# Pieces of weight forms moved into the first half of each plain chunk of a spectral block with a GeGLU FFN

## The chip, the cores and the metric

The kernel runs on one core of one Trainium2 chip. The core has five engines that run their own queues of instructions in order and meet through semaphores: TensorE (PE in the profile, with its weight loads as PEld), VectorE (DVE), ScalarE (ACT), GpSimd (POOL) and SyncE (SP), which here only issues DMAs. The metric is the device time of one execution in microseconds (us), the median of several runs. The three runs shown of the kernel before took 1930.48 to 1935.18 us.

## What is computed

One block of a network with two residual branches, over 8192 tokens of 448 channels:

```python
x = A_x
mod = (_silu(c) @ w_mod).reshape(c.shape[0], 6, 1, -1)
sa, ca, ga, sb, cb, gb = (mod[:, 0], mod[:, 1], mod[:, 2], mod[:, 3], mod[:, 4], mod[:, 5])
h = _layernorm(x, axis=-1) * (1 + ca) + sa
x = x + ga * _A_ref(h, A_w1, A_b1, A_w2, A_b2)
h = _layernorm(x, axis=-1) * (1 + cb) + sb
x = x + gb * _B_ref(h, B_w_gate, B_w_up, B_w_down)
return x
```

`_A_ref` is a spectral layer: a two-dimensional Fourier transform over tokens, a small complex two-layer network on blocks of 112 channels, soft shrinkage, and the inverse transform. `_B_ref` is the FFN, `(_gelu(x @ w_gate) * (x @ w_up)) @ w_down`, with 1792 hidden features. The change touches only the FFN's part of the program.

## The kernel before

**Stages.** First come the layernorm, the transforms and the spectral network (to about 387 us of the profiled execution). Then the FFN runs over 32 chunks of 256 tokens (two groups of 128, `CB = 2`). The first eight, chunks 0 to 7 (`NSTD = 8`), are the *plain chunks*; chunks 8 to 31 use a scheme with seven products in place of eight for a 2x2 block product in gate and up as well, and need other *forms* of the gate and up weights: sums and differences of blocks, each as a high and a low half-precision part. The weights have seven tiles (`NP = 7`), and in plain chunk 1 + n the forms of tile n are built, piece by piece, between the chunk's own work.

**A plain chunk** has 14 steps (k = 0 to 13, `NFT = 14`). In each, `gate_up(i, k)` (L1118 for its matmuls) writes one bank of PSUM, and `gate_up_out` empties it: ScalarE takes the gelu of the gate half (L1154), VectorE multiplies it with the up half (L1159), and that multiply frees the bank. Banks go in pairs of two steps (`pgu`, tags `pa` and `pb`, two buffers each), so four steps are in flight. After each second step GpSimd makes four sums of the product (`sums`, L1167 to L1170), and `quantize` makes its high part on ScalarE (L1178) and the low part on VectorE (L1179). Behind step 2 stand the *down products* of the chunk before (`down`: L1191 to L1193, 147 matmuls in seven products): ScalarE copies two of them out (L1218, L1224), VectorE adds the others (L1219, L1227, L1228, L1232, L1233, L1238), and GpSimd finishes the chunk from L1234 on (L1205, L1206). `down` calls a hook `mid` at three places among the products, written m0, m1, m2 in the tables.

**The next chunk but one is prepared in the same steps** (tables `hooks`, and `soon` for chunks 6 and 7): step 3 splits its spectral values and transform (`split_g`, `split_v`: L113 on ScalarE, L115 on GpSimd); step 6 does the inverse transform on TensorE (`inverse`: L1018 to L1020, of which L1020 needs the last split, `v`); step 7 the residual (`residual`: L1029 on VectorE, L1030 on GpSimd); then the statistics (L1038, L1041), the reciprocal root (L124 to L133), the normalise (`norm2`: L1067, L1068) and the pack (L1073, L1080 to L1082). For chunks 8 and 9 the pack is another: `token_sums` (L1294 to L1300), `wpack_hi` on ScalarE (L1321) and `wpack_lo` on GpSimd (L1327).

**The forms of a weight tile**, by the table `prep`: `load_forms` fetches the raw weights (`wr`, L1513); `form_sums` makes two pairs of sums on GpSimd (part 0: L1522 and L1523; part 1: L1525 and L1526, which overwrites what some pieces read); ten pieces follow, each `forms_hi` on ScalarE (L1556) and `forms_lo` on VectorE (L1561), piece 4 with one more copy (L1564); `store_forms` writes the result (`ws`) to memory in two parts, four DMAs each (L1570). The order on each engine is the order in which the tables call these functions (a schedule written by hand), so an engine waits at the first instruction that is not ready.

**The change of stage.** Behind chunk 7 the plain stage's memory and PSUM pools are closed. The first matmuls of the new stage (L1350, tile `set`) wait until all plain banks are free; then `copy_b` on ScalarE (L1378, tile `sb`) copies their result, and the next matmuls wait for that copy.

Of the kernel before, what the change touches and what calls it, by code (L numbers as in the profile page):

```python
# [32 lines left out]
NFT = F // 128  # L33
# [7 lines left out]
NSTD = 8  # L41
# [8 lines left out]
def spectral_geglu(ctx, tc, x, w1, b1, w2, b2, wg, wu, wd, cvec, wmod, cf1, cs2, cmi, cgm, out):  # L50
# [91 lines left out]
    with ExitStack() as actx:  # L142
# [147 lines left out]
        pe, start = 0.0, {}  # L290
# [684 lines left out]
    with ExitStack() as cctx:  # L975
# [342 lines left out]
        def wpack_hi(i, ks):  # L1318
            for k in ks:
                for src, hi, _ in pieces(i, k):  # L1320
                    S.copy(hi, src)  # L1321
# [111 lines left out]
        held = []  # L1433
# [61 lines left out]
            6: [(2, wpack_hi, [4]), (2, wpack_lo, [4]), (3, load_g)],  # L1495
        }

        def pack(i):
            pack_hi(i)
            pack_lo(i)  # L1500
# [65 lines left out]
        def store_forms(t, part):  # L1566
            w = raws.pop(("s", t, part))
            for pr, rows in enumerate(rows2):
                for r, c in zip(rows2, range(2)):
                    dma(wk[t][part][r, pr], w[rows, :, c::2])  # L1570

        prep = {}
        for n in range(NP):
            for k, fn, *args in (
                (0, load_forms),
                ("m0", form_sums, 0),
                ("m0", forms_hi, 0),
                ("m1", forms_lo, 0),
                ("m1", forms_hi, 2),
                ("m2", forms_lo, 2),  # L1580
                ("m2", forms_hi, 1),
                (3, forms_lo, 1),
                (4, forms_hi, 3),
                (5, forms_lo, 3),
                (5, forms_hi, 4),
                (6, forms_lo, 4),
                (7, form_sums, 1),
                (7, forms_hi, 5),
                (8, forms_lo, 5),
                (8, forms_hi, 6, 7),  # L1590
                (8, store_forms, 0),
                (9, forms_lo, 6, 7),
                (10, forms_hi, 8),
                (11, forms_lo, 8),
                (11, forms_hi, 9),
                (12, forms_lo, 9),
                (13, store_forms, 1),
            ):
                at_k = (n, NFT - 1) if k == 0 and n else (1 + n, k)
                prep.setdefault(at_k, []).append((fn, n, *args))  # L1600
        for n, k in enumerate((4, 7, 11, 13)):
            for part in range(2):
# [10 lines left out]
            11: [(2, norm2, 0)],  # L1613
            12: [(2, norm2, 1)],
            13: [(2, pack)],
        }

# [6 lines left out]
        }  # L1624

        soon = {
            5: [(1, turn)],
            3: [(2, split_g), (2, split_v)],
            6: [(2, inverse)],
            7: [(2, residual)],  # L1630
            8: [(2, stats2), (2, rsqrt_part, 5)],
            9: [(2, rsqrt_part, 9), (2, norm2, 0)],
            10: [(2, norm2, 1), (2, token_sums, 0), (2, wpack_hi, [0, 1]), (2, wpack_lo, [0, 1])],
            11: [(2, token_sums, 1), (2, wpack_hi, [2]), (2, wpack_lo, [2])],
            12: [(2, wpack_hi, [3]), (2, wpack_lo, [3])],
            13: [(2, wpack_hi, [4]), (2, wpack_lo, [4])],
        }

        ahead = {
# [110 lines left out]
        for u in range(U0, NT_ + 1):  # L1750
            period(u)
            i, k = divmod(u, NP)
# [95 lines left out]
```

## Time and profile before

| what | value |
|---|---|
| runs shown, median (lowest to highest) | 1933.28 us (1930.48 to 1935.18) |
| the profiled execution, its own time | 1934.03 us |
| its span, first to last instruction | 1931.7 us |
| mean granted clock of TensorE | 0.989 |
| TensorE busy | 1862.0 us (96%) |
| VectorE, ScalarE, GpSimd busy | 1417.0, 995.3, 1261.5 us |
| plain chunks (first to last L1118) | 386.8 to 790.0 us |
| chunks 8 to 31 | from 798.1 us on |

How to read it: the profile counts an engine as busy while it executes, not while it waits; instructions have the line of the kernel that issued them. In the order of time a row gives start, duration, engine, line, operation, what it writes and reads, and in brackets how long the engine idled before it and what ended that. A row of a table by stage gives the stretch, its length, busy time and count of instructions for PE, PEld, DVE, ACT and POOL, the clock granted to TensorE, the DMA share and GB/s. Chunk numbers are worked out from the order: 308 matmuls of L1118 make one plain chunk.

### The profile page before, as it was taken

To read this page: it belongs to the slowest core of one execution; us is meant where nothing else is said; L and a number is where in the kernel's file an instruction comes from. 1 tells how busy PE (TensorE), PEld (TensorE's weight loads), DVE (VectorE), ACT (ScalarE), POOL (GpSimd) and SP (SyncE) were. 2 spreads that over 40 slices of the span, in tenths; PEclk is the share of its full clock that TensorE was granted. 3 is DMA by queue.
4 is the path that set the end of the run, shared out by engine and by line. 5 is a ranking of instruction groups with operands and counts; after the bars stand their busy time and mean duration, and the time that the engine had idled before them with its cause. 6 is when DMAs were issued, how large, how long until landed. Compare 5 with 4: busy or idle time off the path is not lost.

```text
span 1931.7 us, 56478 instructions
## 1 busy us (share of the span) xinstructions
PE 1862.0 (96%) x23332; PEld 1757.8 (91%) x23332; DVE 1417.0 (73%) x2888; ACT 995.3 (52%) x1843; POOL 1261.5 (65%) x1616
## 2 busy tenths in 40 slices
PE   7899999899999999799999999999999999999998
PEld 3599999778888887699999999999999999999998
DVE  8677788777555565577777777777777777777645
ACT  5687888553333333344444555555555555454443
POOL 3157654247777776577777777777777777777533
PEclk9899999999999999899999999999999999999999
DMA  9999777553434444976665666666565666666651
GB/s 351 315 286 259 200 185 195 163 138 79 101 100 101 100 101 111 247 192 171 168 164 165 164 173 181 169 181 180 167 165 164 164 167 182 168 178 178 157 160 53
DMA packets 380602, 330.49 MB, mean 171 GB/s; under 512 B 110772, under 2 KB 358712, under 8 KB 380344
## 3 DMA queue, kind: packets, MB, share of 16 engines
q1 hardware_dynamic: 380344, 326.87, 61.3%
q8 instruction: 183, 3.00, 0.6%
q14 instruction: 75, 0.61, 0.1%
HBM read 243.32 MB, written 60.10 MB: 157 GB/s over the span
## 4 chain that ended last, share of the span: by engine, by line
PE 72%; DVE 14%; DMA 4%; ACT 4%; POOL 3%; issue 2%; SPq 1%; ACTq 0%; POOLq 0%; DVEq 0%
PE set L1350 36%; PE pdn L1193 6%; PE pdn L1191 6%; PE pdn L1192 6%; PE pgu L1118 4%; PE ps L210 2%; PE set L1193 2%; PE set L1192 2%; PE set L1191 2%; DVE y L471 2%; DVE ws L1561 1%; DVE ac L1179 1%; DVE x L1159 1%; POOL x L1030 1%; DVE wk L824 1%
## 5 line engine op out<-in xcount | busy, mean ns | idle before, releaser
L1350 PE MATMUL set<-nt,wk 128*128 128x128 f16 x13104 | 745.4, 219 | 12.7 <-DVE x L1159 8.1
L1350 PEld LDWEIGHTS <-wk 128*128 128x128 f16 x13104 | 738.3, 98 | 17.9 <-issue 15.9
L1193 PE MATMUL pdn<-wd,ac 128*128 128x224 f16 x1218 | 315.5, 259 | 1.7 <-DVE ac L1425 1.2
L1191 PE MATMUL pdn<-wd,ac 128*128 128x224 f16 x1218 | 315.7, 259 | 0.8 <-ACT ac L1415 0.6
L1192 PE MATMUL pdn<-wd,ac 128*128 128x224 f16 x1218 | 315.5, 259 | 0.0
L1118 PE MATMUL pgu<-nt,wk 128*128 128x256 f16 (+1 forms) x2464 | 274.6, 275 | 19.0 <-DVE x L1159 18.9
L1118 PEld LDWEIGHTS <-wk 128*128 128x128 f16 (+1 forms) x2464 | 227.1, 98 | 65.1 <-issue 38.5
L1399 ACT ACTIVATE gl<-c,dg 128x384 f32<-128x384 f32 x168 | 103.5, 616 | 254.4 <-DVE c L1393 253.3
L1425 DVE SCALAR_TENSOR_TENSOR ac<-x,sa_act,ac 128x896 f16<-128x896 f32 x168 | 212.5, 1265 | 14.8 <-ACT ac L1415 14.7
L1167 POOL TENSOR_TENSOR x<-x 128x128 f32<-128x128 f32 x223 | 135.4, 607 | 122.0 <-DVE x L1159 82.9
L1234 POOL TENSOR_TENSOR o<-u,p 128x224 f32<-128x224 f32 x32 | 21.1, 659 | 278.5 <-DVE u L1233 278.5
L1403 DVE TENSOR_TENSOR x<-c,gl 128x384 f32<-128x384 f32 x168 | 176.2, 1049 | 17.1 <-ACT gl L1399 17.1
L1415 ACT ACTIVATE ac<-x,sa_act 128x896 f16<-128x896 f32 x168 | 173.7, 1034 | 3.5 <-DVE x L1170 0.4
L1170 POOL TENSOR_TENSOR x<-x 128x128 f32<-128x128 f32 x223 | 171.3, 768 | 0.0
L1191 PEld LDWEIGHTS <-ac 128*128 128x128 f16 x1568 | 153.4, 98 | 5.7 <-issue 4.7
L1193 PEld LDWEIGHTS <-ac 128*128 128x128 f16 x1568 | 153.4, 98 | 2.7 <-DVE ac L1425 1.7
L1192 PEld LDWEIGHTS <-ac 128*128 128x128 f16 x1568 | 153.5, 98 | 0.4 <-issue 0.4
L1169 POOL TENSOR_TENSOR x<-x 128x128 f32<-128x128 f32 x223 | 146.3, 656 | 0.0
L1387 DVE TENSOR_TENSOR c<-set,sb 128x512 f32<-128x512 f32 x168 | 115.0, 685 | 42.5 <-PE set L1350 42.5
L1168 POOL TENSOR_TENSOR x<-x 128x128 f32<-128x128 f32 x223 | 117.3, 526 | 17.5
L471 DVE SCALAR_TENSOR_TENSOR y<-pm,t 64x224 f32<-64x224 f32 x256 | 99.5, 389 | 39.0 <-ACT t L463 35.1
L115 POOL TENSOR_TENSOR yl<-y,yh 128x448 fp32r<-128x448 f32 x63 | 76.7, 1218 | 73.5 <-ACT yh L113 60.2
(323 smaller groups left out, 3948.4 us busy)
## 6 DMA issues: line engine op xcount, KB each, us to landing
wk<-wk SPq DMA_DIRECT2D x76, 1024.0 KB, 6.4
wk<-wk SPq DMA_DIRECT2D x76, 768.0 KB, 5.0
tr<-td SPq DMA_DIRECT2D x64, 224.0 KB, 4.6
vd<-us SPq DMA_DIRECT2D x64, 224.0 KB, 3.1
xx<-in_A_x SPq DMA_DIRECT2D x32, 448.0 KB, 4.9
v<-vd SPq DMA_DIRECT2D x63, 224.0 KB, 4.8
out<-x SPq DMA_DIRECT2D x31, 448.0 KB, 4.1
xt<-in_A_x SPq DMA_DIRECT2D x15, 896.0 KB, 16.4
```

The costliest lines, as they stand in the source:

```text
L471: V.scalar_tensor_tensor(y[ri * 64 : ri * 64 + 64, gi], pv[si, ri], LAM, tv[si, ri], op0=ALU.add, op1=ALU.min)
L1118: T.matmul(pgu[i, t, q][:, pr * H : (pr + 1) * H], ws[rows, n, w, tw], nts[i][rows, tn, :], start=start, stop=stop, skip_group_check=True,)
L1167: e.tensor_tensor(s1, a21, a22, ALU.add)
L1169: e.tensor_tensor(s3, a11, a21, ALU.subtract)
L1170: e.tensor_tensor(s4, a12, s2, ALU.subtract)
L1191: T.matmul(ps, ac[:, 0, ka], w[:, 0, kb], start=n == 0, stop=False)
L1192: T.matmul(ps, ac[:, 0, ka], w[:, 1, kb], start=False, stop=False)
L1193: T.matmul(ps, ac[:, 1, ka], w[:, 0, kb], start=False, stop=n == NP - 1)
L1350: T.matmul(ps2[:, pr, reg * 128 : reg * 128 + 128], slot[:, pr, hl, wt, :], nt[:, xt, :], start=start and j == 0, stop=j == len(terms) - 1 ...
L1403: V.tensor_tensor(xs[u][:, 1::3, :], cts.pop(u)[:, 1], gls.pop(u), ALU.mult)
L1415: S.activation(ac[:, 0], xs[u][:, 0:7], AF.Copy, scale=sa_act[:, t : t + 1])
L1425: V.scalar_tensor_tensor(ac[:, 1], xs.pop(u)[:, 0:7], sa_act[:, t : t + 1], ac[:, 0], op0=ALU.mult, op1=ALU.subtract)
```

## The change

The table `prep` is split in two, `start` for tile 0 (in chunk 1) and `steady` for tiles 1 to 6 (in chunks 2 to 7). In `steady` the raw weights are loaded at step 8 of the chunk before (six steps before its end) in place of step 13; the first form sums stand at step 0, the pieces 0 and 2 at steps 0 to 2, pieces 1, 3, 4 and 5 at the hooks m0 to m2 among the down products, the second form sums at m2, and the rest at steps 3 to 6; the stores move from steps 8 and 13 to 3 and 7. For chunks 8 and 9 (table `soon`) the normalise moves to steps 10 and 11, the token sums and the first pack pieces to 12 and 13, and `pack_rest` packs the last two pieces, for chunk 9 in the first period of the new stage.

```diff
+        def pack_rest(i):
+            if i == NSTD:
+                wpack_hi(i, [3, 4])
+                wpack_lo(i, [3, 4])
+            else:
+                held.extend([(f, i, [k]) for k in (3, 4) for f in (wpack_hi, wpack_lo)])
...
+        start = [
+            (0, load_forms),
+            ("m0", form_sums, 0),
+            ("m0", forms_hi, 0),
+            ("m1", forms_lo, 0),
+            ("m1", forms_hi, 2),
+            ("m2", forms_lo, 2),
+            ("m2", forms_hi, 1, 3),
+            (3, forms_lo, 1, 3),
+            (3, forms_hi, 4),
+            (4, forms_lo, 4),
+            (4, form_sums, 1),
+            (4, forms_hi, 5),
...
+            (8, forms_lo, 9),
+            (9, store_forms, 1),
+        ]
+        steady = [
+            (-6, load_forms),
+            (0, form_sums, 0),
+            (0, forms_hi, 0),
+            (1, forms_lo, 0),
+            (1, forms_hi, 2),
+            (2, forms_lo, 2),
+            (2, forms_hi, 1),
+            ("m0", forms_lo, 1),
+            ("m0", forms_hi, 3, 4),
+            ("m1", forms_lo, 3),
+            ("m1", forms_hi, 5),
+            ("m2", forms_lo, 4, 5),
+            ("m2", form_sums, 1),
+            ("m2", forms_hi, 6, 7),
+            (3, store_forms, 0),
+            (3, forms_lo, 6, 7),
+            (4, forms_hi, 8),
+            (5, forms_lo, 8),
+            (5, forms_hi, 9),
+            (6, forms_lo, 9),
+            (7, store_forms, 1),
+        ]
         prep = {}
         for n in range(NP):
-            for k, fn, *args in (
-                (0, load_forms),
-                ("m0", form_sums, 0),
-                ("m0", forms_hi, 0),
-                ("m1", forms_lo, 0),
-                ("m1", forms_hi, 2),
-                ("m2", forms_lo, 2),
-                ("m2", forms_hi, 1),
-                (3, forms_lo, 1),
-                (4, forms_hi, 3),
-                (5, forms_lo, 3),
-                (5, forms_hi, 4),
-                (6, forms_lo, 4),
-                (7, form_sums, 1),
-                (7, forms_hi, 5),
-                (8, forms_lo, 5),
-                (8, forms_hi, 6, 7),
-                (8, store_forms, 0),
-                (9, forms_lo, 6, 7),
-                (10, forms_hi, 8),
-                (11, forms_lo, 8),
-                (11, forms_hi, 9),
-                (12, forms_lo, 9),
-                (13, store_forms, 1),
-            ):
-                at_k = (n, NFT - 1) if k == 0 and n else (1 + n, k)
+            for k, fn, *args in steady if n else start:
+                at_k = (n, NFT + k) if type(k) is int and k < 0 else (1 + n, k)
...
         soon = {
...
-            9: [(2, rsqrt_part, 9), (2, norm2, 0)],
-            10: [(2, norm2, 1), (2, token_sums, 0), (2, wpack_hi, [0, 1]), (2, wpack_lo, [0, 1])],
-            11: [(2, token_sums, 1), (2, wpack_hi, [2]), (2, wpack_lo, [2])],
-            12: [(2, wpack_hi, [3]), (2, wpack_lo, [3])],
-            13: [(2, wpack_hi, [4]), (2, wpack_lo, [4])],
+            9: [(2, rsqrt_part, 9)],
+            10: [(2, norm2, 0)],
+            11: [(2, norm2, 1)],
+            12: [(2, token_sums, 0), (2, wpack_hi, [0, 1]), (2, wpack_lo, [0, 1])],
+            13: [(2, token_sums, 1), (2, wpack_hi, [2]), (2, wpack_lo, [2]), (2, pack_rest)],
         }
```

In the changed kernel the same operations have other line numbers: the pieces are L1563 (ScalarE) and L1568 (VectorE) with the copy L1571, the form sums L1529, L1530 and L1532, L1533. Three places show how the order moves.

VectorE in chunk 4, from the fifth down product (`u`) to step 3, before (`ws` are the pieces, `o` and `u` the down products, `x` the gate/up product, `ac` its quantised form):

```order
L1228 TENSOR_TENSOR u_8613<-pdn,u_8612 128x224
L1561 SCALAR_TENSOR_TENSOR ws<-wr,sww,ws 128x3x128
L1232 TENSOR_TENSOR o<-pdn,u_8613 128x224
L1233 TENSOR_TENSOR u_8612<-pdn,u_8612 128x224
L1238 TENSOR_TENSOR o<-pdn,u_8613 128x224
L1159 TENSOR_TENSOR x_8608<-pgu,gel 128x2x128
L1179 SCALAR_TENSOR_TENSOR ac<-x_8574,sa_act,ac 128x896
L1561 SCALAR_TENSOR_TENSOR ws<-wr,sww,ws 128x128
```

and in the changed kernel:

```order
L1228 TENSOR_TENSOR u_8622<-pdn,u_8621 128x224
L1568 SCALAR_TENSOR_TENSOR ws<-wf,sww,ws 128x3x128
L1571 COPY ws<-ws 128x2x384
L1568 SCALAR_TENSOR_TENSOR ws<-wr,sww,ws 128x3x128
L1232 TENSOR_TENSOR o<-pdn,u_8622 128x224
L1233 TENSOR_TENSOR u_8621<-pdn,u_8621 128x224
L1238 TENSOR_TENSOR o<-pdn,u_8622 128x224
L1159 TENSOR_TENSOR x_8615<-pgu,gel 128x2x128
L1179 SCALAR_TENSOR_TENSOR ac<-x_8579,sa_act,ac 128x896
L1568 SCALAR_TENSOR_TENSOR ws<-wr,sww,ws 128x128
L1568 SCALAR_TENSOR_TENSOR ws<-wr,sww,ws 128x256
```

Ahead of L1232, whose follower L1233 GpSimd's finish needs, stand two pieces and a copy in place of one piece, and step 3 has two pieces in place of one.

GpSimd in chunk 4 at step 7, before (`x` of L1167 to L1170 is the gate/up product, `x` of L1030 the residual of chunk 6):

```order
L1167 TENSOR_TENSOR x_8925<-x_8925 128x128
L1168 TENSOR_TENSOR x_8925<-x_8925 128x128
L1169 TENSOR_TENSOR x_8925<-x_8925 128x128
L1170 TENSOR_TENSOR x_8925<-x_8925 128x128
L1525 TENSOR_TENSOR wr<-wr,wf 128x384
L1526 TENSOR_TENSOR wf<-wr,wf 128x384
L1030 TENSOR_TENSOR x_3369<-x_3369,xx 128x448 x2
```

and, in the changed kernel, first the place that these sums have now, among the down products, and then step 7:

```order
L1532 TENSOR_TENSOR wr<-wr,wf 128x384
L1533 TENSOR_TENSOR wf<-wr,wf 128x384
L1234 TENSOR_TENSOR o<-u_8621,p_8620 128x224
L1205 TENSOR_TENSOR o<-o,gb_r 128x448
L1206 TENSOR_TENSOR x_3369<-o,x_3369 128x448
```

```order
L1167 TENSOR_TENSOR x_8943<-x_8943 128x128
L1168 TENSOR_TENSOR x_8943<-x_8943 128x128
L1169 TENSOR_TENSOR x_8943<-x_8943 128x128
L1170 TENSOR_TENSOR x_8943<-x_8943 128x128
L1030 TENSOR_TENSOR x_3369<-x_3369,xx 128x448 x2
```

The second pair of form sums has gone from between the product sums and the residual add to the place ahead of the finish.

ScalarE at the end of chunk 7, up to the copy of the new stage, before (`gel` is the gelu, `pk` the pack, `sb` the copy):

```order
L1321 CAST pk<-n_11181 128x256
L1154 ACTIVATE gel<-pgu,dg 128x256
L1321 CAST pk<-tf 128x2x192
L1154 ACTIVATE gel<-pgu,dg 128x256
L1178 ACTIVATE ac<-x_11250,sa_act 128x896
L1321 CAST pk<-tf 128x2x256
L1178 ACTIVATE ac<-x_11293,sa_act 128x896
L1378 COPY sb<-set_11348 128x512
```

and in the changed kernel:

```order
L1321 CAST pk<-n_11213 128x256
L1154 ACTIVATE gel<-pgu,dg 128x256
L1178 ACTIVATE ac<-x_11246,sa_act 128x896
L1321 CAST pk<-n_11213 128x256
L1178 ACTIVATE ac<-x_11284,sa_act 128x896
L1321 CAST pk<-tf 128x2x192
L1321 CAST pk<-tf 128x2x256
L1378 COPY sb<-set_11343 128x512
```

The two pack copies that read the token sums (`tf`) now stand behind the last quantise, directly ahead of the copy.

More of the change, by code (lines that the diff above doesn't have):

```diff
@@ L1570, in store_forms @@
                     dma(wk[t][part][r, pr], w[rows, :, c::2])
+        start = [
[11 more added lines that the diff above has]
+            (4, forms_hi, 5),
+            (5, forms_lo, 5),
+            (5, forms_hi, 6, 7),
+            (5, store_forms, 0),
+            (6, forms_lo, 6, 7),
+            (6, forms_hi, 8),
+            (7, forms_lo, 8),
+            (7, forms_hi, 9),
+            (8, forms_lo, 9),
+            (9, store_forms, 1),
+        ]
@@ L1626, in spectral_geglu @@
         soon = {
+            3: [(2, split_g), (2, split_v)],
             5: [(1, turn)],
-            3: [(2, split_g), (2, split_v)],
             6: [(2, inverse)],
```

## The prediction

> **What bounds the kernel now.** I read the page first, then the busy times by stage, then the waits of the plain chunks, then the order of time at three places.
>
> ```profile
> PE 1862.0 (96%) x23332; PEld 1757.8 (91%) x23332; DVE 1417.0 (73%) x2888; ACT 995.3 (52%) x1843; POOL 1261.5 (65%) x1616
> ```
>
> TensorE is the bound, so only its idle time (70 us of 1932) and time at a low clock can be won. Busy time by stage, with the granted clock third from the end:
>
> ```profile
> 612.00:664.00 52.00, 49.82 (x466) 43.80 (x465) 32.08 (x62) 20.66 (x38) 37.36 (x46) 1.00 0.40 95
> 715.00:766.00 51.00, 46.56 (x417) 40.32 (x416) 30.05 (x63) 17.45 (x35) 33.62 (x46) 0.93 0.37 93
> 766.00:804.00 38.00, 25.91 (x236) 22.05 (x235) 28.06 (x54) 15.98 (x30) 28.00 (x37) 0.91 0.88 243
> 804.00:1000.00 196.00, 195.41 (x2953) 193.36 (x2953) 146.21 (x280) 96.10 (x185) 141.54 (x185) 0.99 0.67 181
> 735.96:742.79 6.83, 5.46 (x28) 3.66 (x28) 6.73 (x13) 4.27 (x9) 6.40 (x11) 0.50 0.00 1
> ```
>
> A plain chunk (first row) idles 2.2 us; the last two plain chunks lose 4.4 and 12.1 (51.00 less 46.56, 38.00 less 25.91); behind them TensorE is full (195.4 of 196), so what the plain chunks win stays won. The last row is 6.83 us at half clock inside chunk 6. The waits from 459 to 804 us (total, times, longest) say who holds TensorE:
>
> ```profile
> DVE cst L1038 <- POOL x L1030: 20.3, 14, 3.1
> ACT p L1218 <- PE pdn L1193: 16.2, 6, 4.0
> PE pgu L1118 <- DVE x L1159: 16.1, 19, 2.1
> ```
>
> All 19 waits are for VectorE's multiply (L1159), which reads a gate/up bank and so frees it; VectorE stands in its turn behind GpSimd's residual add (L1030). The order of time in the second half of chunk 4:
>
> ```profile
> 615.71 0.50 DVE L1564 COPY ws<-ws 128x768 f16<-128x768 f16 x1
> ...
> 617.66 1.15 DVE L1179 SCALAR_TENSOR_TENSOR ac<-x,sa_act,ac 128x896 f16<-128x896 f32 x1 [0.51 <-ACT ac L1178]
> 617.77 1.36 POOL L1168 TENSOR_TENSOR x<-x 128x128 f32<-128x128 f32 x1
> ...
> 619.09 0.45 POOL L1169 TENSOR_TENSOR x<-x 128x128 f32<-128x128 f32 x1
> ...
> 619.92 1.34 POOL L1525 TENSOR_TENSOR wr<-wr,wf 128x384 f32<-128x384 f32 x1
> ...
> 621.33 1.00 POOL L1526 TENSOR_TENSOR wf<-wr,wf 128x384 f32<-128x384 f32 x1
> ...
> 622.29 2.22 POOL L1030 TENSOR_TENSOR x<-x,xx 128x448 f32<-128x448 f32 x2
> ...
> 625.30 0.72 DVE L1159 TENSOR_TENSOR x<-pgu,gel 128x256 f32<-128x256 f32 x2
> ...
> 631.53 4.96 PE L1118 MATMUL pgu<-nt,wk 64*128 64x256 f16 x45 [0.93 <-DVE x L1159]
> ...
> 637.29 2.34 PE L1118 MATMUL pgu<-nt,wk 128*128 128x256 f16 x20 [0.80 <-DVE x L1159]
> ```
>
> GpSimd does the second pair of form sums (L1525, L1526) between its product sums and the residual add, so the statistics, and with them the multiply at 625.30, come 2.4 us late (619.92 to 622.29). VectorE then catches up through pieces of forms and the normalise, and TensorE pays 0.93 and 0.80.
>
> **The change, part by part.** *Second halves of chunks 1 to 7.* The form sums leave the place ahead of L1030: the statistics start 2.4 us sooner. Of the five pieces that VectorE had from step 8 on (0.7 us each by the groups quoted for the end of chunk 7, so 3.5) none is left there. The longest wait is 2.1 us, less than the 2.4 alone, so I take all 16.1 us as gone; for none of it to go the residual add would have to come as late as now.
>
> *The half clock of chunk 6.* It follows its three waits. TensorE was busy 5.46 us at 0.50, which is 2.73 us at full clock: 2.7 us won if the waits go (0 if two of them stay). In the Trainium skill, "TensorE: Matmul & The Clock Gate", Part 1, the gate falls to half rate after about one idle window of 3.4 us; here no single wait in chunk 6 is longer than 2.1 us and the clock fell all the same, so waits add up within a window. By the page's rule none of the 2.7 us hangs on these short waits and the sum below would be 13.0, 1920.3; by the row they do, and it is 15.7.
>
> *The end of chunk 7.* The change of stage, in order of time, and then VectorE's groups from 783.8 to 798.1 us (total, mean):
>
> ```profile
> 785.08 4.96 PE L1118 MATMUL pgu<-nt,wk 64*128 64x256 f16 x45 [1.34 <-DVE x L1159]
> ...
> 797.67 0.60 ACT L1321 CAST pk<-tf 128x512 f16<-128x512 f32 x1
> ...
> 798.12 3.22 PE L1350 MATMUL set<-nt,wk 128*128 128x128 f16 x32 [8.08 <-DVE x L1159]
> ...
> 801.30 1.04 ACT L1178 ACTIVATE ac<-x,sa_act 128x896 f16<-128x896 f32 x1 [3.04 <-POOL x L1170]
> ...
> 803.79 0.59 ACT L1378 COPY sb<-set 128x512 f32<-128x512 f32 x1 [1.45 <-DMA wk<-ws]
> ...
> 804.43 1.86 PE L1350 MATMUL set<-nt,wk 128*128 128x128 f16 x16 [3.09 <-ACT sb L1378]
> ```
>
> ```profile
> L1561 DVE SCALAR_TENSOR_TENSOR ws<-wr,sww,ws 128x128 f16<-128x128 f32 (+2 forms) x3 | 2.0, 697 | 0.0
> ...
> L1561 DVE SCALAR_TENSOR_TENSOR ws<-wf,sww,ws 128x384 f16<-128x384 f32 x1 | 0.7, 706 | 0.0
> ...
> L1298 DVE TENSOR_TENSOR tf<-n,tf 128x192 f32<-128x192 f32 x1 | 0.6, 603 | 0.0
> L1299 DVE TENSOR_TENSOR tf<-n,tf 128x192 f32<-128x192 f32 x1 | 0.5, 493 | 0.0
> ```
>
> TensorE ends the plain work at 790.04 (785.08 + 4.96) and waits 8.08 us for the last multiply, until 798.1. VectorE has no gap there (0.0 in each group), so its lateness is the sum of its work. The change takes 2.4 us away at the start of it and the pieces (2.0 + 0.7), and puts token sums behind the last multiply (0.6 + 0.5): 798.1 − 6.2 = 791.9; I take 792.3, for the last gelu now stands behind two pack copies. TensorE itself ends 1.34 us sooner, at 788.7 (that wait is in the 16.1): a wait of 3.6 in place of 8.08. The second wait, 3.09, is for ScalarE's copy L1378, held by the landing of the last form store. That store moves to step 7. But ScalarE's queue ahead of the copy gains two pack copies (0.60 each, the nearest row): the last quantise comes 3.2 us behind the last multiply (801.30 less 798.1), so 792.3 + 3.2 + 1.04 + 1.2 + 0.59 = 798.3, against the end of the first matmuls at 792.3 + 3.2 = 795.5: 2.8 us. Together 11.2 − 6.4 = 4.8 won; bounds 0 (the queue takes it all back) and 9.
>
> *The price: the inverse.* The pieces now stand among the down products. The end of chunk 6's down products, and the inverse in chunk 4:
>
> ```profile
> 701.58 0.39 DVE L1228 TENSOR_TENSOR u<-pdn,u 128x224 f32<-128x224 f32 x1 [1.62 <-PE pdn L1193]
> 701.88 0.61 DVE L1561 SCALAR_TENSOR_TENSOR ws<-wr,sww,ws 128x384 f16<-128x384 f32 x1
> 703.59 0.39 DVE L1232 TENSOR_TENSOR o<-pdn,u 128x224 f32<-128x224 f32 x1 [1.09 <-PE pdn L1193]
> ...
> 704.42 0.66 POOL L1234 TENSOR_TENSOR o<-u,p 128x224 f32<-128x224 f32 x1 [4.58 <-DVE u L1233]
> ```
>
> ```profile
> 610.75 2.09 POOL L115 TENSOR_TENSOR v<-v,vh 128x896 fp32r<-128x896 f32 x1
> ...
> 612.05 1.74 DVE L1179 SCALAR_TENSOR_TENSOR ac<-x,sa_act,ac 128x896 f16<-128x896 f32 x1 [0.51 <-ACT ac L1178]
> ...
> 612.90 0.47 PE L1020 MATMUL pi<-v,gh 128*128 128x448 f32 x1
> ```
>
> From L1234 on GpSimd works without a gap through the finish, the sums and the splits, and its last split ends at 612.84, just as TensorE needs it (612.90). There is no slack: what delays L1234 stops TensorE in step 6. In front of L1232 now stand two pieces and the copy: 0.61 + 0.50 + 0.61 = 1.7 us from 701.97, where 1.6 are free: 0.1 late, the lower end. But the second form sum (1.00 us, L1526) becomes ready at the same moment on GpSimd. The row at 617.77 shows what that means: 1.36 us for an add that takes 0.45 in the row behind it, since it stands beside the quantise of 617.66. If the second piece stands behind the sum, L1234 comes 1.1 late; one more small piece in step 3 adds up to 0.7; and if the split (610.75) comes 1.3 us late, the quantise of 612.05 is ahead of it and costs the 1.15 of such a one more. Range 0.1 to 3.0 a chunk; I take 1.25, nearest to the row of the shared add. In six chunks 7.5, with 0.4 in chunk 1 7.9.
>
> "SBUF — State Buffer", Who interferes with whom, in the Trainium skill has it that a VectorE instruction with two SBUF inputs and a GpSimd one that reads SBUF exclude each other for a whole instruction. By that rule the sum and the pieces queue up, 1.1 us a chunk: 7.0 with chunk 1, and 1916.7 in the end; without it 0.1 a chunk, 1.0, and 1910.7. The 1.36 us speak for the rule.
>
> *At no cost.* Two pieces move to steps 1 and 2. What VectorE does next there is to read the first down products, for which ScalarE too waits 2.7 us a chunk (16.2 in 6, the row for L1218); without that cover they cost 1.4 us a chunk. SyncE's queue moves as well: the loads of the raw weights, and the stores, four issues in 3.39 us:
>
> ```profile
> 689.90 1.74 SPq L1513 DMA_DIRECT2D wr<-in_B_w_gate  x2
> ```
>
> ```profile
> 697.74 1.03 POOL L1522 TENSOR_TENSOR wr<-wr 128x384 f32<-128x384 f32 x1 [1.51 <-DMA wr<-in_B_w_up]
> ```
>
> ```profile
> 797.79 3.39 SPq L1570 DMA_DIRECT2D wk<-ws  x4
> ```
>
> From issue to use a load takes 7.8 us; it is now issued at step 8, six steps of 2.3 us (the row of 637.29) ahead of its use, behind a store of step 7 that can wait only for a piece of step 6. The store at step 3 holds up the output and the transposes of steps 4 and 5 by its 3.4 us; those are used only in the next chunk. The down products' banks are drained by L1227 and L1228 ahead of the new pieces, so no product waits.
>
> **The sum.** 16.1 + 2.7 + 4.8 − 7.9 = 15.7 us. The profiled execution took 1934.03 us (span 1931.7), so 1918.3; the median shown is 0.75 lower: 1917.6.
>
> **The rivals.** (1) *GpSimd is hardly late* (0.1 to 0.5 a chunk): 20 to 23 won, 1910 to 1913. For it: 1.6 of 1.7 us are free; against it the shared add. (2) *The split loses its turn to the quantise, and the change of stage gives nothing*: 2.4 a chunk, 14.8; 16.1 + 2.7 − 14.8 + up to 5 = 4 to 9 won, 1924 to 1929. Against it: the quantise itself waits for sums on GpSimd, so it is late as well. (3) *GpSimd becomes the bound of the plain chunk*: the split comes 3.0 us late in each of six chunks (18.4 with chunk 1), and the residual add, which loses 2.4 us of sums ahead of it, then comes 0.6 later than now behind the same multiplies, so that the 16.1 and the 2.7 stay: 18.4 − 4.8 = 13.6 lost, 1947. It decides from the split coming more than 1.3 us late. For it: no slack at 612.84. Against it: GpSimd is idle for 14.6 us of a chunk (52.00 less 37.36), and a TensorE that waits in step 6 shifts the multiplies as well. (4) *Nothing shows*: the residual add comes as late as now, for GpSimd has been shifted as a whole; then only 0 to 4 are won, 1930 to 1935.
>
> **How the numbers follow.** Forecast (1913 to 1923) 0.50, rival 1 0.20, rival 2 0.18, rival 3 0.05, rival 4 0.07. Faster by over 0.2% (3.9 us, about what a measurement can tell from no change): 0.88; within it 0.07; slower 0.05. The range leaves out rivals 3 and 4 and the far end of rival 2, and goes 2 us below rival 1 for the bound of 9 at the stage's change: 1908 to 1928.
>
> **What would show it.** Right: no wait of TensorE for L1159 over 0.3 us in chunks 2 to 6; L1030 directly behind L1170; full clock from 735 on; the copy behind the stage's change held by ScalarE's queue, not by a store; a new wait of about 1.2 us at L1018 to L1020 for GpSimd's split in each chunk from 2 on. Wrong: the waits for L1159 still there, ScalarE idle at step 0 for raw weights, or a product waiting for a bank.

## The result, and the profile after

The changed kernel takes 1911.81 us, the median of four runs (1909.50 to 1912.27), against 1934.23 (1930.48 to 1935.57) for the kernel before in the same comparison: a ratio of 0.9885, 95% interval 0.9868 to 0.9902, or 22.4 us less. Run once more, beside two of the later experiments, it took 1911.91 (ratio 0.9891, 0.9876 to 0.9906). The predicted time was 1917.6 with a range of 1908 to 1928. The profiled execution took 1911.48 us (span 1909.7), 22.55 less than that of before.

The busy times at the head of the page, after:

```profile
PE 1858.1 (97%) x23332; PEld 1756.6 (92%) x23332; DVE 1433.6 (75%) x2888; ACT 995.4 (52%) x1843; POOL 1264.3 (66%) x1616
```

TensorE is still the bound, with 51.6 us idle in place of 69.7. Where the idle time went is in the busy times of one stretch (length, then busy time of PE, PEld, DVE, ACT and POOL, the granted clock third from the end), from the first gate/up product of chunk 0 to the first product of the next stage, before:

```profile
386.86:798.12 411.26, 383.51 (x3547) 333.81 (x3544) 267.06 (x521) 168.19 (x296) 280.19 (x347) 0.98 0.44 113
```

and after:

```profile
384.88:773.83 388.95, 378.05 (x3546) 332.47 (x3544) 283.70 (x517) 167.51 (x293) 281.24 (x343) 1.00 0.47 120
```

The stretch is 22.3 us shorter: 16.85 of it is idle time of TensorE (27.75 to 10.90), 5.46 is busy time. Ahead of it, in code that the change does not touch, the profiled execution is 2.0 us shorter; behind it 2.3 longer. Of the 2.3, 0.5 is the longer second wait at the change of stage (below), and some 1.7 a fall of the clock near the end (1894.43 to 1897.84 us, TensorE busy 3.41 us at 0.50) that neither the trace of before nor the repeat of the changed kernel has. The start of this stretch lies anywhere from 384.5 to 388.3 us in the profiled executions of this study, so the sections below compare stretches and waits, not starts.

The waits of TensorE from 387 to 815 us (total, times, longest), before:

```profile
PE pgu L1118 <- DVE x L1159: 18.9, 21, 2.6
PE set L1350 <- DVE x L1159: 8.1, 1, 8.1
PE set L1350 <- ACT sb L1378: 3.1, 1, 3.1
```

and after:

```profile
PE set L1350 <- DVE x L1159: 3.8, 1, 3.8
PE pi L1020 <- POOL v L115: 3.6, 7, 0.6
PE set L1350 <- ACT sb L1378: 3.6, 1, 3.6
PE pgu L1118 <- DVE x L1159: 2.6, 1, 2.6
PE pdn L1193 <- DVE ac L1179: 0.6, 1, 0.6
```

The only wait for the multiply L1159 that is left inside the plain chunks is the one of chunk 0, which was there before (2.6). New are seven waits of about 0.5 us at L1020 for GpSimd's split. The second half of chunk 4, after, in order of time:

```profile
605.90 15.34 PE L1118 MATMUL pgu<-nt,wk 128*128 128x256 f16 x141
...
611.58 0.45 POOL L1170 TENSOR_TENSOR x<-x 128x128 f32<-128x128 f32 x1
611.99 2.22 POOL L1030 TENSOR_TENSOR x<-x,xx 128x448 f32<-128x448 f32 x2
```

The residual add follows the product sum directly; 2.4 us of form sums stood between them before. TensorE's run of gate/up products has no gap.

What the change costs is seen in chunk 6, from the down products to the inverse:

```profile
688.57 0.39 DVE L1228 TENSOR_TENSOR u<-pdn,u 128x224 f32<-128x224 f32 x1 [1.62 <-PE pdn L1193]
...
689.63 1.10 POOL L1533 TENSOR_TENSOR wf<-wr,wf 128x384 f32<-128x384 f32 x1 [3.69 <-DVE ws L1568]
...
689.80 1.35 DVE L1568 SCALAR_TENSOR_TENSOR ws<-wr,sww,ws 128x384 f16<-128x384 f32 x1
...
691.07 0.38 DVE L1232 TENSOR_TENSOR o<-pdn,u 128x224 f32<-128x224 f32 x1
...
691.89 0.66 POOL L1234 TENSOR_TENSOR o<-u,p 128x224 f32<-128x224 f32 x1 [1.16 <-DVE u L1233]
...
700.73 2.09 POOL L115 TENSOR_TENSOR v<-v,vh 128x896 fp32r<-128x896 f32 x1
...
701.37 2.40 DVE L1179 SCALAR_TENSOR_TENSOR ac<-x,sa_act,ac 128x896 f16<-128x896 f32 x1 [0.50 <-ACT ac L1178]
...
702.88 0.47 PE L1020 MATMUL pi<-v,gh 128*128 128x448 f32 x1 [0.53 <-POOL v L115]
```

The piece of 689.80 takes 1.35 us beside the form sum of 689.63, so L1234 starts 3.32 us behind L1228; before it was 2.84 (701.58 to 704.42). The split is 0.5 us late for TensorE. It kept its turn: the quantise of 701.37, which began behind it, ended behind it too and took 2.40 us.

The change of stage, after:

```profile
773.83 2.67 PE L1350 MATMUL set<-nt,wk 128*128 128x128 f16 x32 [3.83 <-DVE x L1159]
...
777.58 1.04 ACT L1178 ACTIVATE ac<-x,sa_act 128x896 f16<-128x896 f32 x1 [2.98 <-POOL x L1170]
778.53 1.01 ACT L1321 CAST pk<-tf 128x384 f16<-128x384 f32 x2
...
779.45 0.57 ACT L1378 COPY sb<-set 128x512 f32<-128x512 f32 x1
...
780.07 6.11 PE L1350 MATMUL set<-nt,wk 128*128 128x128 f16 x64 [3.58 <-ACT sb L1378]
```

The first wait is 3.83 in place of 8.08; the second, 3.58, is now for a copy that stands in ScalarE's queue behind a quantise and two packs, not behind a landing store. The repeat of the changed kernel has 3.85 and 2.67 there, with 3.57 us of matmuls between them in place of 2.67: there the clock fell to half before these matmuls began (774.73 against 776.01 us), here while they ran (774.85). The second set starts 6.24 us behind the first in both, so the clock decides how that time splits into work and wait.

### The profile page after: what moved, and what is told of

The parts are those of the page before. It is cut to its first block, busy times and chain, and to the rows that moved or that the text cites. A ratio compares the mean times of both kernels' runs of the same rounds, so it can differ in the third digit from the quotient of the medians.

```text
span 1909.7 us, 56500 instructions
## 1 busy us (share of the span) xinstructions
PE 1858.1 (97%) x23332; PEld 1756.6 (92%) x23332; DVE 1433.6 (75%) x2888; ACT 995.4 (52%) x1843; POOL 1264.3 (66%) x1616
## 4 chain that ended last, share of the span: by engine, by line
PE 78%; DVE 7%; POOL 5%; DMA 4%; issue 3%; ACT 2%; SPq 1%; ACTq 0%; POOLq 0%; DVEq 0%
PE set L1350 38%; PE pgu L1118 8%; PE pdn L1193 6%; PE pdn L1191 6%; PE pdn L1192 6%; PE set L1191 2%; PE set L1193 2%; PE set L1192 2%; PE ps L210 2%; DMA xt<-in_A_x 2%; DVE y L471 1%; POOL v L115 1%; DMA s<-cs 1%; POOL yl L115 1%; PE set L1460 1%
## 5 line engine op out<-in xcount | busy, mean ns | idle before, releaser
L1193 PE MATMUL pdn<-wd,ac 128*128 128x224 f16 x1218 | 316.4, 260 | 1.8 <-DVE ac L1425 1.2
L1118 PE MATMUL pgu<-nt,wk 128*128 128x256 f16 (+1 forms) x2464 | 268.2, 274 | 2.7 <-DVE x L1159 2.6
L1118 PEld LDWEIGHTS <-wk 128*128 128x128 f16 (+1 forms) x2464 | 225.7, 98 | 43.7 <-issue 17.9
L1167 POOL TENSOR_TENSOR x<-x 128x128 f32<-128x128 f32 x223 | 136.3, 611 | 118.2 <-DVE x L1159 50.7
L1234 POOL TENSOR_TENSOR o<-u,p 128x224 f32<-128x224 f32 x32 | 21.0, 658 | 260.6 <-DVE u L1233 260.6
L1170 POOL TENSOR_TENSOR x<-x 128x128 f32<-128x128 f32 x223 | 170.6, 765 | 0.1
L1193 PEld LDWEIGHTS <-ac 128*128 128x128 f16 x1568 | 153.6, 98 | 2.8 <-DVE ac L1425 1.7
L1154 ACT ACTIVATE gel<-pgu,dg 128x256 f32<-128x256 f32 x112 | 49.9, 471 | 158.3 <-PE pgu L1118 148.3
```

What stands on the lines that cost most here:

```text
L1118: T.matmul(pgu[i, t, q][:, pr * H : (pr + 1) * H], ws[rows, n, w, tw], nts[i][rows, tn, :], start=start, stop=stop, skip_group_check=True,)
L1167: e.tensor_tensor(s1, a21, a22, ALU.add)
L1170: e.tensor_tensor(s4, a12, s2, ALU.subtract)
L1193: T.matmul(ps, ac[:, 1, ka], w[:, 0, kb], start=False, stop=n == NP - 1)
```

## The experiments

Each is told as an edit of the changed kernel. Times are medians; the ratio is to the kernel before.

**What held the multiply: the form sums on GpSimd, or the pieces on VectorE?** The first run puts the second form sums back at step 7, with only the two pieces that need them:

```diff
-            ("m2", form_sums, 1),
...
+            (7, form_sums, 1),
+            (7, forms_hi, 8),
+            (8, forms_lo, 8),
+            (8, forms_hi, 9),
+            (9, forms_lo, 9),
+            (10, store_forms, 1),
```

> As the changed kernel, but the second pair of form sums back at step 7 ahead of the residual add, with the two pieces that need it (8 and 9) right behind, at steps 7 to 9; the other three of the moved pieces stay early. Theory (GpSimd's sums are the cause): the statistics come 2.3 us late again and waits for L1159 come back in each of chunks 1 to 7, 0.5 to 1.5 us of idle a chunk in place of none, while the wait at L1020 falls from 0.5 to under 0.2; net 3 to 10 us slower than the changed kernel, 1915 to 1922. Rival (VectorE's pieces behind the residual add are the cause, five of them before, two here): hardly any waits for L1159, and with the 0.5 at L1020 gone 1907 to 1911.

It took 1922.72 us (0.9944, 0.9929 to 0.9959), just past the theory's 1915 to 1922 and far from the rival's. The order of time from the end of chunk 4 to the start of chunk 5:

```profile
616.60 0.99 POOL L1533 TENSOR_TENSOR wf<-wr,wf 128x384 f32<-128x384 f32 x1
...
617.55 2.54 POOL L1030 TENSOR_TENSOR x<-x,xx 128x448 f32<-128x448 f32 x2
...
626.92 1.25 PE L1118 MATMUL pgu<-nt,wk 64*128 64x256 f16 x11 [0.74 <-DVE x L1159]
```

Of the 19 waits for L1159 nine are back (6.2 us from 459 us on), one more of 1.4 us at the start of chunk 7 is put down to the landing of a form store, which this edit moves to step 10, and those at L1020 are gone from chunk 2 on. The second run does the reverse, sums early and five pieces late:

```diff
-            ("m1", forms_hi, 5),
-            ("m2", forms_lo, 4, 5),
+            ("m2", forms_lo, 4),
             ("m2", form_sums, 1),
-            ("m2", forms_hi, 6, 7),
...
+            (7, forms_hi, 5),
+            (8, forms_lo, 5),
...
+            (12, forms_lo, 9),
+            (13, store_forms, 1),
```

> As the changed kernel, with the second pair of form sums early (among the down products), but the five pieces 5 to 9 back at steps 7 to 12, behind the residual add. Theory (GpSimd's sums are the cause): no waits for L1159 over 0.3 us in chunks 1 to 6; the wait at L1020 smaller than 0.5; behind chunk 7 the first wait 2 to 4 us longer than the 3.8 of the changed kernel, since 3.5 us of pieces stand ahead of the last multiply; 1911 to 1917. Rival (VectorE's pieces are the cause): waits for L1159 of 1 to 2 us idle a chunk are back, 1920 to 1928.

It took 1914.34 us (0.9903, 0.9888 to 0.9917), as the theory had it, but not for all its reasons: six waits for L1159 of up to 0.7 us (2.9 in all) came, where it expected none over 0.3. The first wait behind chunk 7 is 6.3 us, 2.5 longer than in the changed kernel, within its 2 to 4.

Two plain chunks in a row show the shares. The windows from the first gate/up product of chunk 3 to that of chunk 5, in the sums-late run, the pieces-late run, the kernel before (where the window has the length of these two chunks but starts 2.2 us behind the first product, at equal busy time) and the changed kernel:

```profile
526.60:626.93 100.33, 98.15 (x924) 86.30 (x924) 65.56 (x123) 40.27 (x72) 73.23 (x88) 1.00 0.40 96
```

```profile
525.34:623.67 98.33, 97.09 (x927) 86.27 (x922) 63.69 (x123) 40.53 (x72) 73.19 (x89) 1.00 0.38 99
```

```profile
531.41:633.74 102.33, 97.98 (x925) 86.23 (x923) 62.79 (x123) 40.28 (x72) 72.61 (x89) 1.00 0.38 95
```

```profile
524.27:622.17 97.90, 96.89 (x927) 86.32 (x922) 68.07 (x123) 40.37 (x72) 73.43 (x89) 1.00 0.40 99
```

The shortest that any run reached is 96.9 (below). Over that, before loses 5.4, the sums late (with two pieces) 3.4, five pieces late 1.4, the changed kernel 1.0. The sums on GpSimd are the larger cause (4.0 us between before and the pieces-late run); VectorE's pieces add to it, and with the sums out of the way still cost something. The sums late without any late piece was not run: two pieces need them.

**Pieces or normalise?** The next two take one half of the change each:

```diff
         soon = {
-            9: [(2, rsqrt_part, 9)],
-            10: [(2, norm2, 0)],
...
+            9: [(2, rsqrt_part, 9), (2, norm2, 0)],
+            10: [(2, norm2, 1), (2, token_sums, 0), (2, wpack_hi, [0, 1]), (2, wpack_lo, [0, 1])],
...
```

> The new places of the pieces and form sums, with the normalise steps of chunks 8 and 9 as before. Theory (the second form sums, out of the way of the residual add, are what frees VectorE's multiply L1159; the later normalise only trims the change of stage): no wait of TensorE for L1159 over 0.3 us in chunks 1 to 6, the waits at L1020 for GpSimd's split as in the changed kernel (0.5 us each in seven chunks); behind chunk 7 the two waits together 5 to 9 us, where the changed kernel has 7.4; time 1909 to 1917. Rival (the normalise steps are worth 5 us or more of the gain): the two waits behind chunk 7 stay near 11 us, with new waits for L1159 in chunk 7; 1917 to 1923.

Pieces alone: 1914.92 us (0.9903, 0.9888 to 0.9917), inside the theory's range. The two waits behind chunk 7 are 5.3 and 1.9, together what the changed kernel has; what the old normalise steps bring back is one wait for L1159, 1.6 us, at the start of chunk 7: of the kind that the rival named, but far too small for its 5 us.

```diff
-            for k, fn, *args in steady if n else start:
-                at_k = (n, NFT + k) if type(k) is int and k < 0 else (1 + n, k)
+            for k, fn, *args in (
+                (0, load_forms),
...
+                (13, store_forms, 1),
+            ):
+                at_k = (n, NFT - 1) if k == 0 and n else (1 + n, k)
```

> The new normalise steps of chunks 8 and 9 alone, the pieces and form sums as before. Theory: the waits for L1159 stay in chunks 1 to 5 as before (some 13 of them), the waits at L1020 stay below 0.2 us; only the end of chunk 7 changes, by 1 to 4 us, for the token sums and half of the packs stand behind the last multiply while the five late pieces stay; 1929 to 1934. Rival (normalise worth 5 us or more): 1923 to 1928.

Normalise alone: 1929.75 us (0.9973, 0.9963 to 0.9983; ten runs from 1924.83 to 1931.73). The 19 waits for L1159 are there, 14.3 us; the two at the change of stage are 6.6 and 2.5. The halves add up in the medians: 18.4 and 3.6 us against their kernel before (1933.30), 22.0, and together 22.4. That is weak evidence that they are independent, for the ten runs of the normalise alone spread over 7 us, and the half clock of 735.96 to 742.79 us is missing from the traces of both halves.

**The price at L1020.** If it is the sum beside a piece, either moving the sum alone or ending it sooner removes it. First the sum behind the splits, with pieces 4 and 5 left where they are:

```diff
-            ("m2", form_sums, 1),
             ("m2", forms_hi, 6, 7),
...
+            (4, form_sums, 1),
+            (5, forms_hi, 8),
...
+            (8, store_forms, 1),
```

> As the changed kernel, but the second pair of form sums stands at step 4, behind GpSimd's splits for the inverse, with pieces 8 and 9 at steps 5 to 7; pieces 4 and 5 stay between the down products. Theory (the wait at L1020 comes from the sum running beside VectorE's pieces, which then hold back L1232, L1233 and GpSimd's L1234): the waits at L1020 fall from 0.5 us to under 0.2 in chunks 2 to 7, 3 to 4 us won; but the residual add comes 0.5 to 1.2 us later, which may bring back small waits for L1159 (0 to 0.7 a chunk); 1907 to 1913. Rival (the pieces alone, 1.7 us in front of L1232 where 1.6 are free, and the additional one in step 3, make the split late): the waits at L1020 stay at 0.4 to 0.5; 1911 to 1916.

It took 1909.91 us (0.9876, 0.9859 to 0.9892). In chunk 6:

```profile
687.77 0.39 DVE L1228 TENSOR_TENSOR u<-pdn,u 128x224 f32<-128x224 f32 x1 [1.62 <-PE pdn L1193]
...
689.00 0.61 DVE L1568 SCALAR_TENSOR_TENSOR ws<-wr,sww,ws 128x384 f16<-128x384 f32 x1
...
689.78 0.39 DVE L1232 TENSOR_TENSOR o<-pdn,u 128x224 f32<-128x224 f32 x1 [0.17 <-PE pdn L1193]
...
690.62 0.66 POOL L1234 TENSOR_TENSOR o<-u,p 128x224 f32<-128x224 f32 x1 [5.74 <-DVE u L1233]
```

With the same two pieces and the copy in front of L1232 the second piece takes 0.61 us in place of 1.35, L1232 waits for TensorE (0.17) and not the reverse, L1234 starts 2.85 us behind L1228 as before, and the wait at L1020 is gone from chunk 2 on. The rival, pieces alone, falls. Of 3 us won, two waits for L1159 (1.0 us) take a part back, and so does the change of stage: from the last plain product to the second set it lasts 10.7 us in place of 10.1. Then piece 4 and the sum one place sooner, into a gap that GpSimd has anyway (3.69 us in front of 689.63 above):

```diff
-            ("m1", forms_lo, 3),
+            ("m1", forms_lo, 3, 4),
+            ("m1", form_sums, 1),
             ("m1", forms_hi, 5),
-            ("m2", forms_lo, 4, 5),
-            ("m2", form_sums, 1),
+            ("m2", forms_lo, 5),
```

> As the changed kernel, but in the steady table piece 4 (and its copy) and the second form sums stand one place sooner, behind the second group of down products, so that the sum on GpSimd runs in its idle stretch ahead of L1228 and not beside the pieces in front of L1232. Theory (sum beside pieces): the waits at L1020 go in chunks 2 to 7 (under 0.15 us), no wait for L1159 comes; 3 to 4.5 us won, 1907 to 1909. Rival (GpSimd's finish and the one additional piece in step 3 make the split late by themselves): 0.3 to 0.5 stay at L1020, 1910 to 1912.

It took 1909.17 us (0.9872, 0.9857 to 0.9887), 2.6 less than the changed kernel and just outside the 1907 to 1909 that the theory gave. The waits at L1020 from 459 to 815 us, and two plain chunks of it:

```profile
PE pi L1020 <- POOL v L115: 0.5, 1, 0.5
```

```profile
525.54:622.45 96.91, 96.86 (x926) 86.36 (x922) 65.98 (x123) 40.41 (x72) 74.06 (x89) 1.00 0.40 100
```

In these two chunks TensorE is idle for 0.05 us: they have no idle time left to win. Against the changed kernel's 97.90 the price was 0.5 us a chunk. The one wait left at L1020 is that of chunk 1, which has the other table.

**The change of stage.** ScalarE's copy of the first set goes ahead of the last quantise and the held packs:

```diff
+            if u == U0:
+                copy_b(u)
+                quantize(NSTD - 1, NP - 1)
             for fn, *args in held:
                 fn(*args)
...
-            on(u, copy_b)
+            if u > U0:
+                on(u, copy_b)
...
-        quantize(NSTD - 1, NP - 1)
```

> As the changed kernel, but at the change of stage ScalarE's copy of the first set (L1378) is issued ahead of the last quantise of chunk 7 and of the held packs. Theory (the second wait, 3.58 us, is ScalarE's queue: the copy stands behind a quantise that waits for GpSimd's sums and behind two pack casts): the wait falls to 0.3 to 1.0 us; the first, 3.83, stays; the clock is back to full some 7 us sooner; 3 to 5 us won, 1906 to 1909. Rival (it is only moved: the quantise and the packs are needed soon behind, and TensorE waits for them in the first periods instead): the second wait falls, new waits of 2 us or more come in periods 1 to 3; 1910 to 1913.

It took 1907.25 us (0.9865, 0.9850 to 0.9879), 4.6 less than the changed kernel. TensorE at the change of stage:

```profile
778.00 3.13 PE L1350 MATMUL set<-nt,wk 128*128 128x128 f16 x32 [3.85 <-DVE x L1159]
781.80 2.55 PE L1350 MATMUL set<-nt,wk 128*128 128x128 f16 x42 [0.67 <-ACT sb L1378]
784.87 1.33 PE L1350 MATMUL set<-nt,wk 128*128 128x128 f16 x21 [0.52 <-ACT set L1382]
```

The second wait fell from 3.58 to 0.67 and no wait of 2 us came behind it. From the last plain product to the second set TensorE takes 7.6 us in place of 10.1, and in the trace the half clock behind it lasts 3.41 us (2.74 of work) in place of 10.24 (6.66 of work), which wins some 2.0 us more. The first wait, 3.85, looked like 1.6 us of chunk 9's normalise ahead of the last multiplies, so the next two runs kept the copy first and issued that normalise behind the multiplies; the second of them also put its packs one period later:

```diff
+                    if i == NSTD - 1 and k >= 11:
+                        if fn is pack_rest:
+                            pack_rest(i + d)
+                        else:
+                            held.append((fn, i + d, *args))
```

> As the run with the copy first, and in chunk 7 the second half of chunk 9's normalise, its token sums and packs are issued behind the last multiply too. Theory (the first wait, 3.83 us, is the sum of VectorE's work ahead of the last two multiplies, 1.6 us of it the normalise of 770.65 and 771.56): it falls to 1.9 to 2.5 us, and the clock does not fall to half, or for one window of 3.4 us at most; 1.5 to 4 us more than the run with the copy first, 1903 to 1907. Rival (something else holds the last multiply, the gelu or ScalarE's packs): the first wait stays above 3 us, 1906 to 1910.

```diff
+            packs = [h for h in held if u == U0 and h[0] in (wpack_hi, wpack_lo)]
             for fn, *args in held:
-                fn(*args)
-            held.clear()
+                if (fn, *args) not in packs:
+                    fn(*args)
+            held[:] = packs
```

> As the run with the second half of chunk 9's normalise behind the last multiply, but its packs stand one period later, behind ScalarE's copy L1382 for the second set. Theory (the 6.07 us that TensorE then waited for L1382 were the packs ahead of it on ScalarE, waiting for VectorE's normalise): first wait 1.4 to 1.6 us, second 0.7, third below 1 us, no half clock; 1.9 to 4 us below the run with the copy first, 1903 to 1906. Rival (the quantise that waits for GpSimd's sums holds L1382 as well, or the packs hold the second period): a wait of 2 us or more stays in the first three periods; 1906 to 1911.

The first took 1912.47 us (0.9890, 0.9875 to 0.9905), the second 1910.82 (0.9887, 0.9872 to 0.9902): the one past both ranges, the other in its rival's. The first wait fell to 1.46 in both (1.9 to 2.5 expected of the first run, 1.4 to 1.6 of the second), but what was put off came due within 12 us. In the first:

```profile
783.08 8.94 PE L1350 MATMUL set<-nt,wk 128*128 128x128 f16 x112 [6.07 <-ACT set L1382]
```

and in the second:

```profile
779.23 2.18 POOL L115 TENSOR_TENSOR v<-v,vh 128x896 fp32r<-128x896 f32 x1
...
779.40 2.22 DVE L1298 TENSOR_TENSOR tf<-n,tf 128x192 f32<-128x192 f32 x1
...
781.66 0.51 ACT L1321 CAST pk<-tf 128x384 f16<-128x384 f32 x1 [2.44 <-DVE tf L1298]
...
783.00 0.58 ACT L1378 COPY sb<-set 128x512 f32<-128x512 f32 x1
...
783.63 2.61 PE L1350 MATMUL set<-nt,wk 128*128 128x128 f16 x23 [4.70 <-ACT sb L1378]
```

The packs now waited in ScalarE's queue for VectorE's normalise and token sums, and the copies that TensorE needs stood behind them. In the second run one token sum (L1298) stood beside GpSimd's split on top of that: 2.22 us, 0.60 in the changed kernel.

**Both edits in one kernel.** Piece 4 sooner together with the second way of the normalise:

> The change of stage of the run beside it, and piece 4 with the second form sums one place sooner, in one kernel. Theory (the two act in different places and add up): no waits at L1020 in chunks 2 to 7 (3.0 us), and the gain at the change of stage; 1900 to 1904. Rival (they do not add up: what is won in the plain chunks is lost at the change of stage): 1903 to 1908.

1908.81 us (0.9873, 0.9857 to 0.9890): the waits at L1020 are gone from chunk 2 on, that of 4.7 us is there, and the time is past both expectations. Then the two edits that had gained alone, copy first and piece 4 sooner:

> The two edits that gained alone, the copy first at the change of stage and piece 4 with the second form sums one place sooner, and no other. Theory (they act in different places and add up): no waits at L1020 in chunks 2 to 7, 48.4 us a plain chunk, waits of 3.9, 0.7 and 0.5 us at the change of stage; some 7 us below the changed kernel, 1903 to 1906. Rival (the sooner end of the plain chunks lets another wait show at the change of stage, as it did in the run with both and the normalise behind): 1906 to 1910.

1904.66 us (1903.83 to 1904.92; 0.9852, 0.9836 to 0.9869). They add up: 4.6 and 2.6 alone, 7.2 together. That is faster than both kernels. Its waits from 459 to 815 us:

```profile
PE set L1350 <- DVE x L1159: 3.8, 1, 3.8
PE set L1350 <- ACT sb L1378: 0.7, 1, 0.7
PE pdn L1193 <- DVE ac L1179: 0.6, 1, 0.6
PE set L1350 <- ACT set L1382: 0.5, 1, 0.5
```

The run of the changed kernel beside e10 was the measure for it:

> The changed kernel itself once more, as the measure for the two runs beside it on the same chip: 1910 to 1913 by every theory.

It took 1911.91 us, as told at the start.

## Why the prediction was right, and where its sizes were off

Direction and range held. The time lies 5.8 us below the predicted one: outside the forecast's own band of 1913 to 1923 (chance 0.50) and in that of the first rival (0.20). The size missed because two terms were off the same way, the price at the inverse by 4.3 us and the busy time by 2.7, and the change of stage by 1.0 the other way. Step by step (one trace of each kernel):

| term | predicted, us | measured in the profiled execution, us |
|---|---|---|
| waits for L1159 in the plain chunks | 16.1 | 16.3 idle, and 2.7 more of busy time |
| half clock in chunk 6 | 2.7 | 2.7 |
| change of stage | 4.8 | 3.8 |
| price at the inverse | −7.9 | −3.6 |
| sum | 15.7 | 21.9 |

*The waits.* The mechanism was right: all 19 waits from 459 us on are gone (16.3 us counts one more, in chunk 1 ahead of 459), L1030 stands directly behind L1170, and putting the sums back brings nine of the waits back. The claim that the 2.4 us of sums alone explain them was too simple: the pieces-late run still loses 1.4 us in two chunks.

*Their size.* Here a reading of the view failed. The quoted column is idle time. The group of L1118 in the changed kernel:

```profile
L1118 PE MATMUL pgu<-nt,wk 128*128 128x256 f16 (+1 forms) x2464 | 268.2, 274 | 2.7 <-DVE x L1159 2.6
```

A matmul counts as 274 ns of busy time, while 2464 of them fill 268.2 us, 109 ns each: they overlap. So the last one ahead of a wait hides some 0.16 us of it as busy. The two plain chunks of the windows above show it: the kernel before is busy 97.98 us for the products that take 96.86 where nothing waits, 1.1 us in seven waits, 0.16 each. Of the 5.46 us of busy time that the stretch lost, 2.7 is the half clock, and 2.7 is left; this accounts for most of it (14 waits fewer at 0.16 are 2.2, an estimate), the rest is open.

*The half clock.* Right in what became of it. It lay across the start of chunk 7 (first product at 737.34 us before, at 720.07 after) and not inside chunk 6. The stretch of after that holds this place has the full clock, where the same window read 0.93 before:

```profile
715.00:766.00 51.00, 49.85 (x476) 44.02 (x474) 36.73 (x70) 21.34 (x41) 39.86 (x51) 1.00 0.56 146
```

Short waits had brought it down, and it stayed up once they were gone. The prediction's condition, that all would be lost if two of the three waits stayed, was too strict: with the normalise alone moved, two stay (1.02 and 1.38 us), the third is 0.17 in place of 2.08, and the clock stays full. Whether every execution of the kernel before has this fall is not shown; its runs have mean clocks from 0.988 to 0.992.

*The price.* The step that was mis-sized. It had L1234 come 1.1 us late if the piece queues up behind the whole form sum, and took 1.25 a chunk for the split. L1234 came 0.48 late (3.32 less 2.84) and TensorE waits 0.5 us a chunk. The second piece lost 0.74 us beside the sum (1.35 less 0.61), not 1.00, and some 0.2 of that was free. The additional piece in step 3, priced at up to 0.7, showed no wait: in the run with piece 4 sooner it is there and L1020 does not wait. Seven chunks at 0.5 are 3.6 where 7.9 stood. "SBUF — State Buffer", Who interferes with whom, in the Trainium skill has a VectorE instruction with two SBUF inputs and a GpSimd one that reads SBUF exclude each other. The 1.35 and 0.61 agree with that in kind; the price worked out from it, a whole instruction of 1.1 us a chunk, is about twice the 0.5 measured. That a port is the reason is not shown by these runs, only that the two instructions side by side are.

*The change of stage.* Both waits were named rightly, with their causes (the sum of VectorE's work, then ScalarE's queue in place of the store): 3.83 and 3.58 where 3.6 and 2.8 stood, 3.85 and 2.67 in the repeat. With the work between the waits, from the last plain product to the second set, it is 14.4 us before and 10.1 after, 4.3 won where 4.8 stood. The copy-first run shows that the second wait is the queue: 0.67 is left without it.

*The rivals.* GpSimd hardly late, 0.1 to 0.5 a chunk, is what happened, at its upper end. The split did not lose its turn to the quantise (it was the quantise that waited, 2.40 us), GpSimd did not become the bound, and the residual add does not come as late as before. Not foreseen was the wait of 0.6 at L1193 in chunk 7's down products.

## What to carry to other kernels

Read first whose order of work the bounding engine waits on, and move what stands in front of it on the slower helper: here 2.4 us of form sums on GpSimd, ahead of an add, held TensorE by way of VectorE, and moving them was worth more than moving five pieces on VectorE. Put moved work into a gap that the profile shows on its own engine and not beside work that it slows down (a piece of 0.61 us took 1.35 here); one place sooner made the rest of the price vanish. Work that is put off at a change of stage is due soon behind it: an order of the queue in which the copy that frees a bank goes first gained 4.6 us, and putting off what VectorE computes gained nothing.

## What the runs showed of the hardware that was not expected

The granted clock changes in these traces at steps of 3.41 us (it falls for 3.41, 6.83, 10.24 or 13.65 us), and the half clock follows how much of such a stretch TensorE worked, not the length of one wait. Such stretches of the changed kernel at the change of stage (length, PE busy, granted clock third from the end), and then the stretch ahead of the half clock at the start of chunk 7 in the kernel before:

```profile
768.03:771.44 3.41, 1.97 (x19) 1.61 (x17) 3.38 (x6) 1.52 (x5) 1.61 (x2) 1.00 1.07 370
771.44:774.85 3.41, 1.02 (x19) 1.02 (x19) 2.81 (x7) 1.34 (x2) 3.41 (x8) 1.00 1.10 340
774.85:785.09 10.24, 6.66 (x65) 6.50 (x63) 3.48 (x5) 3.98 (x7) 8.02 (x9) 0.50 0.86 276
```

```profile
732.55:735.96 3.41, 1.37 (x12) 0.75 (x10) 3.23 (x9) 1.32 (x4) 0.00 (x0) 1.00 0.00 0
```

Busy for 1.97 us kept the full clock; 1.37 and 1.02 were followed by half. The other stretches of the 14 traces bear that out: cut at the same steps, every stretch at full clock with 1.4 us of work or less was followed by half, every one with 1.8 us or more kept it, and between 1.5 and 1.75 both came (in the changed kernel's trace 1.68 us from 1891.02 lost it, 1.75 from 78.54 kept it). "TensorE: Matmul & The Clock Gate", Part 1, in the Trainium skill gives about one idle window of 3.4 us as the condition of the half rate. These stretches were not idle, and the measurement decides: TensorE busy for 40% of a stretch or less did it here, for 53% or more did not. At the change of stage the changed kernel pays this once, 6.66 us of work at half clock behind chunk 7; its trace has other falls outside of what the change moves, at the start of the FFN (375.50 to 382.33 us) and in chunk 0 (409.63 to 413.04).
